# Filler matmuls of a planned attention and Fourier-mixing kernel: up to the first feed-forward products instead of nearly to the end

## The chip, the cores and the metric

The kernel runs on one core of one Trainium2 chip. Its time is measured on the device in microseconds; the number given is the median of several executions. One execution more is taken with the hardware profiler, and all rows of the profile are of that one.

## The reference

Inputs are q, k, v of shape (8, 12, 448, 64) and two weights, 768 x 3072 and 3072 x 768, in float32.

```python
q_n, k_n = q / |q|, k / |k|                       # along the 64
attn = softmax(q_n @ k_n.T / tau)                 # tau = 0.1
x = (attn @ v)  reshaped to (8, 448, 768)
u = x + real(fft(fft(x, axis=1), axis=2))
un = (u - mean(u)) / sqrt(var(u) + 1e-6)          # along the 768
out = u + relu(un @ w_ch1) @ w_ch2
```

## The kernel before

The kernel is not a loop that engines run through. It is a list of operations, each with the engines that can do it, its assumed duration, its priority, what it reads and writes, and the PSUM tiles that it takes. A planner puts them in order and the order is then written out for each engine, with a semaphore wait wherever an operation needs the result of another engine.

**The stages of a batch.** There are eight batches. For each: q and k rows are loaded into STG (three buffers), squared on ScalarE (L1371), summed on VectorE (L1373), their inverse norms made (L1170 to L1174), scaled on GpSimd into QH (L1384) and transposed by DMA into QK (L1390). Then come the scores (L1461, and L1474 for the rows that remain), the exponentials on ScalarE into E (L1439), the products with v (L1492, L1498) and the division by the row sums on VectorE into X (L1516, L1518). The Fourier transform is folded by its symmetries on VectorE into F and ACG (L1537 to L1589); a first set of products over the 448 rows (L1629) is copied out of PSUM by ScalarE (L1650) and VectorE (L1651), and a second set (L1679, L1682) makes the sums over the 768 columns, which VectorE adds to X to make U (L1713, L1724). Mean and variance follow, the normalized rows are written into F (L1776) and transposed by DMA into UNT (L1797). The feed-forward part multiplies UNT with W1b (the "up" products, named h, L1861), applies relu while it leaves PSUM into HQ (L1877; the first row tile of batch 0 goes into a part of TX), and multiplies with W2b (the "down" products, L2005). VectorE adds U on the way out (L2041, L2042), and SP or GpSimd stores the rows.

**How batches interleave.** Attention of batch b + 1 is listed ahead of the feed-forward part of batch b, and the planner weaves both together: products are put where TensorE would otherwise wait. W1b and W2b are loaded once by GpSimd's DMA queue during batch 0 (L1151, L1152), the 12 slices of W2b one behind the other. In batch 0 the down products of the first row tile run over both halves of the hidden columns, so that the last four of the first output half read the last W2b slice.

**The order.** `Plan.schedule` (L727) goes through simulated time with measured durations, a model of the DMA queues and a safety margin on DMA landings (for the weights, 1.5 us), and picks for each engine in turn the operation that can start first, by priority where several can. The order within an engine is fixed from then on.

**The fillers.** `Plan.fill` (L868) then walks TensorE's finished order. Wherever there is a gap of at least 0.36 us between two operations of the plan, within a stretch of planned time from t0 to t1, it can put in matmuls whose result nobody reads. Each filler is a group of six 128 x 128 x 128 matmuls (L2255), one for each 0.36 us of the gap (0.7 us early in the run), into a PSUM bank that is free in the plan at that time. A filler waits for the last VectorE operation that the plan has done by then, so that it doesn't run long before its time. With a `share` under 1, a gap is filled only where TensorE is busy for less than that share in some 3.4 us stretch around it. Nothing else moves: the order of the real operations stays, and no operation waits for a filler other than by standing behind it in TensorE's order.

`Kern.build` calls it twice (L2259, L2260). The first call goes from 7.5 us of the plan to `first`, the planned start of the first up product of batch 0 (`h0_0`), and multiplies an identity matrix that lies in TX. The second goes on from there and multiplies a piece of W1b, with a share of 0.75.

Of the kernel before, what the change touches and what calls it, by code (L numbers as in the profile page):

```python
# [970 lines left out]
class Kern:  # L971
# [1242 lines left out]
    def build(self):  # L2214
        self.stg_next = self.qh_next = self.ln_next = self.out_next = 0
        self.trs, self.loads, self.ssk, self.fd_ops, self.w, self.raw1, self.vl, self.pvs, self.exps = [], [], [], [], [], [], [], [], []
        self.first_st = self.main = self.last_qk = self.ldt = None
        self.units()
        self.hT0 = self.tf[:, 9216:12288].rearrange("p (f c) -> p f c", f=NF)
        self.snu, self.fs = [], []  # L2220
        self.consts()
        self.tables()
        self.attn(0)
        self.trig.order += tuple(self.exps)
        for b in range(self.nb):
            self.fft(b)
            if b == 0:
                self.weights(self.vl[2])
            if b + 1 < self.nb:
                self.attn(b + 1)  # L2230
            if b == 0:

                for c in range(3):
                    self.w[12 + c].deps.update(self.ssk)
                for c in (3, 4):
                    self.w[12 + c].deps.add(self.sqw)
                for c in range(5, 12):
                    self.w[12 + c].deps.update(self.raw1[3] + (self.raw1[4] if c > 7 else []))
            if b == self.nb - 2:
                self.s1 = []  # L2240
                self.wsums()
            self.ffn(b)
        seen = {}
        for op in self.P.ops:
            k = seen[op.name] = seen.get(op.name, -1) + 1
            op.prio = round(op.prio + SHIFT.get(op.name, {}).get(k, 0), 4)
            op.engs = (HOME[op.name][k],) if k in HOME.get(op.name, ()) else op.engs
        self.est = self.P.schedule()
        first = min(op.start for op in self.P.ops if op.name == "h0_0")

        def warm(w):
            def make(bank):
                def fn(pe):
                    for _ in range(6):
                        r = pe.matmul(self.PS[:, bank, 0:128], w, w, start=True, stop=True)  # L2255
                    return r
                return fn
            return make
        self.P.fill(7.5, first, self.id_op, warm(self.ID))  # L2259
        self.P.fill(first, self.est - 20.0, self.id_op, warm(self.W1b[:, 0, 0:128]), 0.75)  # L2260
        self.P.emit(self.nc, self.es)
        self.es.close()

# [52 lines left out]
```

## Time and profile before

| | us |
|---|---|
| median of 3 runs | 581.55 |
| lowest and highest run | 580.40 and 582.12 |
| the profiled execution | 580.54 |
| its span, first to last instruction | 578.7 |
| granted TensorE clock, mean over the span | 1.00 |
| TensorE matmuls busy | 557.1 |
| VectorE busy | 428.9 |
| ScalarE busy | 394.0 |
| GpSimd busy | 227.5 |

The profile's page gives the busy time of each engine, the span in 40 slices, the DMA queues, the chain of work that ended last, and the costliest groups of instructions. A group's row names line, engine and operation, what it writes and reads (out<-in), its shape and count, then busy time, the mean of one, and the idle time ahead of it with its releaser. In the order of time a row starts with the start and the length in us; what stands in brackets at its end is how long the engine sat idle ahead of it, and for whom. PE is TensorE, PEld its weight loads, DVE VectorE, ACT ScalarE, POOL GpSimd, SP the engine that issues DMAs. Matmuls are pipelined: a row's length runs to the end of its last matmul, and the next row can start before that.

### The profile page before, as it was taken

Reading aid. Unit: us, or ns where it says so; the run is one execution under the profiler, and the core shown is the slowest. Engines: PE = TensorE matmul, PEld = TensorE weight load, DVE = VectorE, ACT = ScalarE, POOL = GpSimd, SP = SyncE. Lnnn points to the kernel's source line nnn. Section 1 sums busy time; section 2 is a strip of 40 time slices with the busy share of each in tenths; the row PEclk is TensorE's granted clock in tenths of the full one; section 3 lists DMA queues with packets and bytes.
Section 4 is the critical chain, followed back from the end, with each engine's and each line's share of the span. In section 5 each row is a group of like instructions: output and inputs, shape, how many; then the busy total and the mean of one; then the engine's idle time right before and its main releaser. Section 6 shows DMA issues by size and latency. Waiting matters only on the chain.

```text
span 578.7 us, 16114 instructions
## 1 busy us (share of the span) xinstructions
PE 557.1 (96%) x6658; PEld 437.6 (76%) x6658; DVE 428.9 (74%) x917; ACT 394.0 (68%) x740; POOL 227.5 (39%) x332
## 2 busy tenths in 40 slices
PE   3899999989999999999999999999999999999997
PEld 3678787667688687868768688687786886969694
DVE  8889958778558957794698668866678469897262
ACT  7998875556777786767748877586565772857270
POOL 8523315157335634543371634645244002031303
PEclk9999999999999999999999999999999999999999
DMA  9999999995449766925495649561490300122001
GB/s 216 195 233 189 167 184 107 131 190 84 110 94 108 165 99 137 144 56 138 79 122 116 105 117 123 114 148 42 84 118 15 84 1 1 57 43 71 28 29 54
DMA packets 183946, 62.19 MB, mean 107 GB/s; under 512 B 166689, under 2 KB 181665, under 8 KB 183873
## 3 DMA queue, kind: packets, MB, share of 16 engines
q0 software_dynamic: 54048, 22.81, 34.7%
q1 hardware_dynamic: 129824, 38.35, 34.1%
q8 instruction: 52, 0.85, 0.6%
q14 instruction: 22, 0.17, 0.1%
HBM read 51.90 MB, written 11.01 MB: 109 GB/s over the span
## 4 chain that ended last, share of the span: by engine, by line
PE 80%; DVE 10%; ACT 4%; DMA 2%; POOL 2%; issue 1%; POOLq 0%; ACTq 0%; DVEq 0%
PE PS L2005 28%; PE PS L1861 27%; PE PS L1956 7%; PE PS L1498 5%; PE PS L1461 5%; ACT E L1439 2%; PE PS L1492 2%; PE PS L1474 1%; PE PS L2255 1%; DMA UNT<-F 1%; DVE SM L1250 1%; PE PS L1682 1%; PE PS L1629 1%; DMA QK<-QH 1%; DVE F L1544 1%
## 5 line engine op out<-in xcount | busy, mean ns | idle before, releaser
L1861 PE MATMUL PS<-UNT,W1b 128*128 128x256 bf16 (+1 forms) x1728 | 185.2, 264 | 3.0 <-DMA UNT<-F 2.2
L1861 PEld LDWEIGHTS PS<-UNT,W1b 128*128 128x128 bf16 x1728 | 153.8, 98 | 23.5 <-DMA UNT<-F 2.6
L1439 ACT ACTIVATE E<-PS 128x900 bf16<-128x900 f32 (+1 forms) x192 | 148.7, 826 | 28.7 <-PE PS L1461 23.4
L2005 PE MATMUL PS<-W2b,HQ 128*128 128x384 bf16 x720 | 125.5, 326 | 0.0
L1384 POOL TENSOR_TENSOR QH<-STG,SM 128x256 bf16<-128x256 f32 x126 | 88.2, 726 | 83.1 <-DVE SM L1174 56.6
L2005 PEld LDWEIGHTS PS<-W2b,HQ 128*128 128x128 bf16 x720 | 68.7, 98 | 43.4 <-issue 0.9
L2031 POOL TENSOR_TENSOR OUTB<-OUTB,U 128x192 f32<-128x192 f32 x72 | 51.9, 742 | 102.6 <-ACT OUTB L2026 100.8
L1877 ACT ACTIVATE HQ<-PS 128x512 bf16<-128x512 f32 x91 | 54.3, 597 | 43.0 <-PE PS L1861 40.6
L2005 PE MATMUL PS<-TX,HQ 128*128 128x384 bf16 (+2 forms) x444 | 76.8, 322 | 2.2 <-DVE OUTB L2042 2.2
L2005 PEld LDWEIGHTS PS<-TX,HQ 128*128 128x128 bf16 x444 | 41.6, 98 | 28.6 <-DVE OUTB L2042 3.6
L2105 DVE TENSOR_TENSOR HQ<-HQ 128x1536 bf16<-128x1536 bf16 (+1 forms) x73 | 52.8, 728 | 13.8 <-ACT HQ L1877 7.7
L1373 DVE TENSOR_REDUCE SM<-QH 128x6 f32<-128x384 f32 x84 | 45.5, 544 | 16.1 <-ACT QH L1371 15.8
L1371 ACT ACTIVATE QH<-STG 128x384 f32<-128x384 f32 x84 | 43.2, 518 | 13.2 <-DVE SM L1373 9.8
L1498 PE MATMUL PS<-VB,E 128*128 128x65 bf16 x1152 | 51.4, 193 | 0.0
L2064 POOL DMA_INDIRECT out_dram<-OUTB,IDX x21 | 22.5, 1073 | 67.6 <-DVE OUTB L2042 27.0
L1498 PEld LDWEIGHTS PS<-VB,E 128*128 128x128 bf16 x1152 | 47.7, 97 | 1.5
L1492 PE MATMUL PS<-VZ,E 128*128 128x130 bf16 x192 | 41.5, 219 | 0.6 <-ACT E L1439 0.5
L1877 DVE TENSOR_SCALAR HQ<-PS 128x512 bf16<-128x512 f32 x35 | 24.1, 688 | 22.6 <-PE PS L1861 22.3
L1416 POOL DMA_DIRECT2D VB<-in_v_dram x24 | 25.5, 1071 | 38.1 <-PE PS L1498 32.1
L1724 DVE SCALAR_TENSOR_TENSOR U<-ACG,X 128x768 bf16<-128x768 f32 (+4 forms) x39 | 39.5, 1020 | 0.8
L1461 PE MATMUL PS<-QK 64*128 64x225 bf16 (+2 forms) x864 | 39.5, 229 | 0.5 <-DMA QK<-QH 0.4
L2026 ACT ACTIVATE OUTB<-PS 128x384 f32<-128x384 f32 x36 | 17.5, 486 | 28.6 <-PE PS L2005 28.3
(193 smaller groups left out, 789.8 us busy)
## 6 DMA issues: line engine op xcount, KB each, us to landing
STG<-in_q_dram SPq DMA_DIRECT2D x18, 384.0 KB, 4.1
STG<-in_k_dram SPq DMA_DIRECT2D x18, 384.0 KB, 3.7
VB<-in_v_dram POOLq DMA_DIRECT2D x24, 192.0 KB, 6.6
W2b<-in_moe_w_ch_dram POOLq DMA_DIRECT2D x12, 384.0 KB, 7.4
W1b<-in_moe_w_ch_dram POOLq DMA_DIRECT2D x5, 768.0 KB, 11.9
out_dram<-OUTB SPq DMA_DIRECT2D x7, 384.0 KB, 3.8
W2b<-in_k_dram SPq DMA_DIRECT2D x2, 576.0 KB, 7.3
W2b<-in_q_dram SPq DMA_DIRECT2D x2, 576.0 KB, 10.1
```

The lines of the kernel that those rows point to most:

```text
L1371: P.add("act", lambda a, sq=sq, src=buf[:, w * x:w * x + w]: a.activation(sq, src, ACTF.Square), t_act(w), pr, f"sq{i}_{b}", reads=bn, wri ...
L1373: P.add("dve", lambda v, o=SS[:, i, H // ns * x:H // ns * (x + 1)], sq=sq: v.tensor_reduce(o, sq.rearrange("p (h d) -> p h d", d=DH), AX.X ...
L1384: r = v.tensor_tensor(v3(qh)[:, h:h + 4], v3(buf)[:, h:h + 4], RN[:, i, h:h + 4].unsqueeze(2).to_broadcast((128, 4, DH)), AluOp.mult)
L1439: return a.activation(o, self.PS[:, bk:bk + nc_, 0:SQ2], ACTF.Exp, scale=1.0 / self.tau)
L1461: i = pe.matmul(self.PS[:, bk + h, c0:c0 + n], self.KT[r, jj, kt * 128:(kt + 1) * 128], self.QT[r, jj, cols], start=True, stop=True)
L1492: r = pe.matmul(o, st(6), self.VZ[:, j, :], start=not split, stop=(split and i == 0), skip_group_check=True)
L1498: r = pe.matmul(o[:, 65 * h:65 * h + 65], st(2 * kt + h), self.VB[:, kt, 2 * j + h, :], start=(split and i == h == kt == 0), stop=((not sp ...
L1861: r = pe.matmul(self.PS[:, bk, x * n:(x + 1) * n], self.W1b[:, j, ft * 128:(ft + 1) * 128], self.UNT[:, j, cs], start=(j == 0), stop=(j == ...
L1877: return e.activation(o, i, ACTF.Relu) if e is self.nc.scalar else e.tensor_relu(o, i)
L2005: r = pe.matmul(self.PS[:, bk, 0:n], lhs(f), rhs(f), start=(start and f == 0), stop=(stop and f == NF // 2 - 1), skip_group_check=True)
L2031: r = g.tensor_tensor(self.OUTB[:, ob, xs], self.OUTB[:, ob, xs], self.U[:, ut, xs], AluOp.add)
L2105: P.add("dve", lambda v: v.tensor_tensor(cs(o), cs(a), cs(bq), op), 0.16 + 0.3 * len(ks), -0.5, f"{nm}{ks[0]}_{b}", reads=rd, writes=[x fo ...
```

## The change

One argument of the second call differs: the end of the stretch of planned time in which fillers may be put.

```diff
@@ -2257,7 +2257,7 @@
                 return fn
             return make
         self.P.fill(7.5, first, self.id_op, warm(self.ID))
-        self.P.fill(first, self.est - 20.0, self.id_op, warm(self.W1b[:, 0, 0:128]), 0.75)
+        self.P.fill(first, first + 12.0, self.id_op, warm(self.W1b[:, 0, 0:128]), 0.75)
         self.P.emit(self.nc, self.es)
         self.es.close()
 
```

`self.est` is the planned end of the last operation. The first call, the order of the real operations and their waits are the same.

## The prediction

> **What bounds the kernel now.** I read the page first, then the fillers' own line, then TensorE's order of time around them, then the chain of waits.
>
> ```profile
> span 578.7 us, 16114 instructions
> PE 557.1 (96%) x6658; PEld 437.6 (76%) x6658; DVE 428.9 (74%) x917; ACT 394.0 (68%) x740; POOL 227.5 (39%) x332
> ...
> PE 80%; DVE 10%; ACT 4%; DMA 2%; POOL 2%; issue 1%; POOLq 0%; ACTq 0%; DVEq 0%
> ```
>
> TensorE is busy for 96% of the span and carries 80% of the chain that ended last. A busy row is not proof of a bound, but the chain says the same: work taken off TensorE shortens the end, unless something else comes late in its place. So the questions are how much filler work really goes, and whether what follows it was ready.
>
> ```profile
> L2255 PE MATMUL PS<-TX x144: 217/219/314, 8.1 to 48.4; 128*128 128x128 bf16 x144
> L2255 PEld LDWEIGHTS PS<-W1b x60: 95/98/99, 93.9 to 97.7; 128*128 128x128 bf16 x60
> L2255 PE MATMUL PS<-W1b x60: 219/219/230, 94.0 to 97.7; 128*128 128x128 bf16 x60
> ```
>
> All fillers of the kernel are these: 144 from the first call (their operand lies in TX) and 60 from the second (operand W1b). The second call reaches nearly to the end of the plan, but it found only one place worth filling, 3.8 us wide, around 94 us.
>
> ```profile
> 48.66 6.81 PE L1861 MATMUL PS<-UNT,W1b 128*128 128x128 bf16 x114
> ```
>
> ```profile
> 92.71 1.46 PE L2005 MATMUL PS<-W2b,TX 128*128 128x384 bf16 x8
> 94.01 3.95 PE L2255 MATMUL PS<-W1b 128*128 128x128 bf16 x60
> 97.80 4.71 PE L2005 MATMUL PS<-W2b,TX 128*128 128x384 bf16 x28
> 102.34 0.56 PE L1629 MATMUL PS<-CS,F 128*97 128x225 bf16 x4
> ...
> 103.93 2.11 PE L2005 MATMUL PS<-W2b,HQ 128*128 128x384 bf16 x12
> 105.88 0.21 PE L1679 MATMUL PS<-CS,E 97*128 97x96 bf16 x1
> ```
>
> The first feed-forward product starts at 48.66 us. The new limit, 12 us later, is 60.7 us, and the 60 fillers lie 33 us beyond it: no disagreement of that size is likely between the plan's clock, in which the limit is counted, and the trace. Between 48.66 and 60.7 there is no filler now, and none can be added, since the lower bound of the stretch is the same. So the change is: all 60 go, nothing comes. The 144 stay. The row of the 28 products has no idle time ahead of it, so TensorE went straight from the fillers to them.
>
> ```profile
> 94.17 0.34 PE PS L2255 x6
> ...
> 94.52 3.44 PE PS L2255 x54
> 97.96 4.55 PE PS L2005 x28
> 102.51 1.58 PE PS L1629 x16
> 104.09 1.95 PE PS L2005 x12
> ```
>
> The chain runs through the fillers: 97.96 - 94.17 = 3.79 us. That is the largest gain, 0.65% of the run. A change of 0.3% (1.74 us) is about what a measurement of this kernel can tell from no change.
>
> **Term 1: were the 28 products ready at 94.01?** They read the last slices of W2b, the results of earlier products, and a PSUM bank.
>
> ```profile
> 86.18 0.71 POOL L1152 DMA_DIRECT2D W2b<-in_moe_w_ch_dram  x1 [8.95 <-DMA W2b<-in_moe_w_ch_dram]
> ```
>
> ```profile
> W2b<-in_moe_w_ch_dram POOLq DMA_DIRECT2D x1, 384.0 KB, 4.5
> ```
>
> ```profile
> 93.00:94.00 1.00, 1.00 (x8) 0.57 (x6) 1.00 (x4) 0.04 (x1) 1.00 (x3) 1.00 0.00 0
> 94.00:95.00 1.00, 0.99 (x15) 0.70 (x14) 0.97 (x3) 0.89 (x2) 0.38 (x1) 1.00 0.00 0
> ```
>
> The twelfth and last W2b load is issued at 86.18 and lands 4.5 us later, at 90.7. The windows say the same (their columns: stretch, length, busy time and count of PE, weight loads, VectorE, ScalarE and GpSimd, granted clock, DMA share, GB/s): the DMA engines moved nothing from 93 to 95 us. So the slice that the planner expected late is there 3.3 us before TensorE reaches the gap. The plan has a wait there of the fillers' length; on the chip it doesn't exist, and the fillers only delay.
>
> ```profile
> 89.08 0.68 DVE L1877 TENSOR_SCALAR HQ<-PS 128x512 bf16<-128x512 f32 x1
> ...
> 97.90 0.64 DVE L1589 TENSOR_TENSOR F<-ACG 128x388 bf16<-128x388 bf16 x2
> ...
> 99.84 0.30 DVE L1174 RECIPROCAL SM<-SM 128x24 f32<-128x24 f32 x1
> ```
>
> The last eviction of a feed-forward bank (L1877) is over by 89.76, so the bank and the operand are free too. Term 1: the 28 products start at 94.01 instead of 97.80, gain 3.79, and end (4.55) at 98.56. What hides the W2b load is the work ahead of 94 us; each microsecond of landing beyond 94.0 would cost one.
>
> **Term 2: the sums of the transform, L1629.** They come next and need the fold that VectorE ends with L1589, at 97.90 + 0.64 = 98.54. VectorE doesn't wait for the fillers (they wait for it), so this time doesn't move.
>
> ```profile
> 41.64 1.27 DVE SM L1250
> 42.95 0.84 PE PS L2255 x12
> ```
>
> The handover from VectorE to TensorE costs 42.95 - 41.64 - 1.27 = 0.04, and a weight load may be uncovered for 0.098. So L1629 starts between 98.56 and 98.54 + 0.14 = 98.68, against 102.34: gain 3.66 to 3.78.
>
> **Term 3: the second transform, L1679.** It needs the evictions of L1629 by ScalarE (L1650) and VectorE (L1651).
>
> ```profile
> 102.55 0.62 DVE L2041 SCALAR_TENSOR_TENSOR OUTB<-PS,MV,U 128x384 f32<-128x384 f32 x1 [2.40 <-PE PS L2005]
> ...
> 103.08 0.54 DVE L1373 TENSOR_REDUCE SM<-QH 128x6 f32<-128x384 f32 x1
> ...
> 103.34 0.92 ACT L1650 ACTIVATE E<-PS 128x900 bf16<-128x900 f32 x1 [3.32 <-PE PS L1629]
> ...
> 104.13 1.09 DVE L1651 CAST E<-PS 97x900 bf16<-97x900 f32 x1 [0.51 <-PE PS L1629]
> ...
> 107.14 1.03 DVE L1713 TENSOR_TENSOR ACG<-PS,ACG 128x388 f32<-128x388 f32 x2 [1.45 <-PE PS L1682]
> ```
>
> VectorE's order behind L1174, which ends at 100.14 by a chain that doesn't hang on the fillers, is L2041, L1373, L1651: 100.14 + 0.62 + 0.54 + 1.09 = 102.39, and with the handover 102.53. TensorE itself would be there at 98.68 + 1.58 + 1.95 = 102.21. So VectorE ends last by about 0.3 us, and L1679 starts at 102.53 against 105.88: gain 3.35 (3.66 if the three overlap as closely as L2041 and L1373 do now). ScalarE has waited 3.32 us for its part and has the room. I take 3.4.
>
> **Term 4: all that follows.** From L1713 on VectorE waits for TensorE again. Its three waits for TensorE in this stretch are 2.40 + 0.51 + 1.45 = 4.36 us, more than the 3.79 removed, so it can follow. The next place where something other than TensorE ends last is this:
>
> ```profile
> 105.31 4.67 SPq L1390 DMA_TRANSPOSE QK<-QH  x2
> ...
> 114.69 5.78 SPq L1797 DMA_TRANSPOSE UNT<-F  x3
> ...
> 122.95 3.23 PE L1861 MATMUL PS<-UNT,W1b 128*128 128x256 bf16 x28 [2.20 <-DMA UNT<-F]
> ```
>
> ```profile
> 111.00:112.00 1.00, 1.00 (x9) 0.61 (x7) 1.00 (x3) 0.39 (x1) 0.00 (x0) 1.00 0.29 61
> 112.00:113.00 1.00, 1.00 (x8) 0.61 (x7) 0.93 (x5) 0.94 (x4) 0.00 (x0) 1.00 0.00 0
> ```
>
> TensorE waits 2.20 us for the transposes of batch 1's normalized rows, which hang on L1713 and so move with it. Issued 3.4 us earlier, at 111.3, they meet an SP queue that is free since 105.31 + 4.67 = 109.98 and DMA engines that fall idle during that very microsecond (0.29 busy, then 0.00). At most 0.3 us is lost; the 2.20 us wait stays as it is. From there on every load is set off by a buffer that comes free, and each engine has waited for TensorE, so all is shifted alike. No wait is added, no DMA is moved; those that hang on TensorE's count behind the gap come earlier with it.
>
> **Sum.** 3.79 less 0.4 is 3.4 us. The profiled execution took 580.54 us (span 578.7 and 1.84 around it) and would take 577.1; it lies 1.0 below the median of the runs, 581.55, which becomes 578.1.
>
> **A rule that speaks against it.** The granted clock is 1.00 in every window above, with the fillers in. But the rows of the start show what fillers are for:
>
> ```profile
> 8.06 2.74 PE L2255 MATMUL PS<-TX 128*128 128x128 bf16 x24 [8.06 <-DVE SM L1250]
> 11.43 1.46 PE L2255 MATMUL PS<-TX 128*128 128x128 bf16 x12 [0.63 <-DVE SM L1173]
> ```
>
> After 8.06 us without work, twelve matmuls take 1.46 us, where the same twelve take 0.84 at 42.95. The Trainium skill, TensorE: Matmul & The Clock Gate, section "Why this matters for your kernels", says that the array must not idle for more than some 3 us between bursts, since one idle window drops its clock to half. By that rule a 3.8 us hole at 94 us would be paid for behind it. The slow rows agree with its direction, though the clock column reads 1.00 there as well. It bites only if the hole stays open, and by term 1 the products close it.
>
> **Rivals.** *Slower: the hole stays open and the clock falls.* Place: 94.0 to 97.8 us. It decides if the last W2b slice lands some 3 us or more after 94.0, that is 6 us later than in the profile; then nothing is gained by the removal, and the matmuls behind run slowly. Price by the start's rows: the slow pace lasted at least from 8.06 to 11.43 + 1.46 = 12.89, 4.83 us, and at 0.84 instead of 1.46 us per twelve they would have taken 2.78, so 2.05 lost: 583.6. For it: the planner did expect to wait. Against: the landing at 90.7, and DMA engines at rest.
>
> *No change: the gain is given back at the UNT transposes.* If those didn't come earlier, because their queue or an engine in front of them keeps its time, TensorE would wait there 2.20 + 3.4 = 5.6 us and the run stay at 581.5; half given back leaves 579.8. For it: this is the one wait of over 2 us behind the gap, so nothing spare covers a delay there. Against: the queue and the engines are free in the rows of term 4.
>
> *The edit does nothing:* it would if the planned place lay within 12 us of the first product; the trace has it 45 us behind. Then 581.55.
>
> **How the numbers follow.** Forecast 0.85 (gain over 1.74 us, most likely 3.4), given back 0.09, no effect 0.02, slower 0.04. So faster 0.85, same 0.11, slower 0.04. The range: full gain of 3.79 with a median as far under as the lowest run shown is now (1.15) gives 576.6; above, half given back with the same median's 0.57 over (the highest run, 582.12) gives 580.4.
>
> **What would show it.** Right: 204 fillers become 144, none behind 48.4; L2005 x28 right after 94.0 without idle time; L1629 near 98.7, L1679 near 102.5 with a short wait for VectorE's L1651, the UNT wait still about 2.2 us at 119.5, granted clock 1.00. Wrong: TensorE idle at 94 to 98 us with products at a slower pace behind it (term 1), a wait for UNT of over 4 us (term 4), or a new wait for QK later that the 3.4 us uncovered.

## The result, and the profile after

| | before | after |
|---|---|---|
| median of all runs, us | 582.02 (17 runs) | 575.65 (17 runs) |
| lowest and highest run | 580.40 and 583.74 | 574.49 and 580.28 |
| the profiled execution | 580.54 | 576.17 |
| after over before | | 0.9898, interval 0.9883 to 0.9913 |

The kernel became faster by 5.9 us (5.1 to 6.8). The forecast had the sign, and the fillers' removal as the forecast described it is there, with 3.7 us. It was too low: it had 3.4 us of gain, and 3.79 as the most that the fillers could give. About 2 us came from a place where it had expected nothing.

The page of after, its first rows: 120 instructions on TensorE fewer, 60 matmuls and their 60 weight loads.

```profile
span 574.2 us, 15994 instructions
PE 553.6 (96%) x6598; PEld 433.3 (75%) x6598; DVE 428.4 (75%) x917; ACT 393.4 (69%) x740; POOL 227.6 (40%) x332
```

The fillers' own line in after: the first call's 144 are left, and none lies behind 48.5 us.

```profile
L2255 PE MATMUL PS<-TX x144: 216/219/314, 8.1 to 48.5; 128*128 128x128 bf16 x144
```

TensorE's order of time in after, around the place (start, length, then in brackets the idle time ahead of the row and its releaser):

```profile
92.72 6.01 PE L2005 MATMUL PS<-W2b,TX 128*128 128x384 bf16 x36
98.61 0.60 PE L1629 MATMUL PS<-CS,F 128*97 128x225 bf16 x4
...
102.21 0.20 PE L1679 MATMUL PS<-CS,E 97*128 97x96 bf16 x1
...
117.42 12.84 PE L1861 MATMUL PS<-UNT,W1b 128*128 128x256 bf16 x116 [0.34 <-DMA UNT<-F]
```

The 8 products ahead of the fillers and the 28 behind them are now one row of 36 without a break. L1629 starts 3.73 us earlier than before (98.61 against 102.34) and L1679 3.67 (102.21 against 105.88). Then comes the row that the forecast didn't have: the products on UNT wait 0.34 us for the transposes, not 2.20, and start 5.53 us earlier than in before (117.42 against 122.95).

**Where the lead grows and shrinks.** All engines execute the same instructions in the same order in both kernels, the 120 apart, so each instruction of TensorE can be set against its twin. The table gives the start in after less the start in before, at five places of before's time, for two profiled executions of after (the second is e7 below):

| at, us of before | after | after again (e7) |
|---|---|---|
| 109.9 | -3.68 | -3.43 |
| 122.95, UNT | -5.53 | -5.27 |
| 139.9, QK | -6.02 | -5.77 |
| 199 | -6.49 | -6.40 |
| the end | -4.47 | -5.55 |

The first row is the fillers. The second adds 1.85 us at the UNT transposes. The third adds 0.5 at a wait for QK transposes which stood in before, in its order of time,

```profile
139.92 0.56 PE L1461 MATMUL PS<-QK 64*128 64x225 bf16 x8 [0.43 <-DMA QK<-QH]
```

and has no idle time in after; the section on more counts comes back to it. Where the 0.5 us between 140 and 199 us come from stays open. Part of the lead is given back later, and not alike in two executions of the same kernel. The largest single piece, in after alone, is this row of its order of time, which e7 does not have:

```profile
233.91 3.67 PE L1861 MATMUL PS<-UNT,W1b 128*128 128x256 bf16 x30 [0.59 <-ACT HQ L1877]
```

**What happened to the 2.20 us.** VectorE and ScalarE work between 107 and 121 us of before's time comes 3.67 to 3.73 us earlier in after, and so do the three transpose issues:

```profile
111.02 5.68 SPq L1797 DMA_TRANSPOSE UNT<-F  x3
```

against 114.69 in before: 3.67. So the issue explains none of the extra 1.85. The landing does. The products wait for one semaphore, that of the second of these transposes, and the chain of before has that wait as a step of its own (start, length):

```profile
117.30 5.60 DMA UNT<-F
```

The second transpose, issued at 117.30, landed at 122.90, and TensorE went on at 122.95. In after it was issued at 113.58 (3.72 us earlier), its semaphore had the last of its 16 updates at 117.38, and TensorE went on at 117.42. From issue to landing it took 5.60 us in before and 3.80 in after: 1.80 us less. The first transpose isn't what TensorE waits for (in before it landed in 2.8 us), and neither is the third (4.45 us, at 123.66, when TensorE had gone on).

What else was on the DMA engines while TensorE stood still? The DMA view of before, from 120.6 to 122.9 us (queue, then packets, MB, share):

```profile
DMA packets 680, 0.19 MB, mean 81 GB/s; under 512 B 679, under 2 KB 679, under 8 KB 679
...
q1 hardware_dynamic: 679, 0.17, 121.4%
q8 instruction: 1, 0.02, 2.5%
```

and of after, in its own stop from 116.9 to 117.4 us:

```profile
DMA packets 422, 0.11 MB, mean 216 GB/s; under 512 B 422, under 2 KB 422, under 8 KB 422
...
q1 hardware_dynamic: 422, 0.11, 113.1%
```

One packet tells them apart: a single 16 KB packet of the queue named "instruction". Both pages have 52 of them:

```profile
q8 instruction: 52, 0.85, 0.6%
```

0.85 MB over 52 is 16384 bytes. The trace has 13,445 records of TensorE in before and 13,325 in after, so one packet is 256 instructions of 64 bytes (52 x 256 = 13,312). In before the first of the 52 begins when TensorE has started 281 instructions and the last when it has started 13,234, which is 254 from one to the next: these are TensorE's instructions being fetched. The Trainium skill, Runtime: NRT & Kernel Launch, section "Instruction fetch mechanics", says that a sequencer refills its buffer in blocks of 16 KiB, 256 instructions, by a DMA queue of its own, and that crossing a block's end is mostly hidden. The block's size agrees with the rows above. What a crossing costs TensorE's own stream no row here shows; the packets below show who else pays.

The trace has every packet. The 256-byte packets of the transposes, from the first UNT issue until TensorE goes on:

```
                        fetch            packets over 0.6 us   they start       they end         longest
before                  120.95-121.89    18 of 2354            121.14-121.27    122.68-122.72    1.56 us
before again (e4)       122.07-123.01    18 of 2352            122.25-122.39    123.80-123.84    1.57 us
after + 120 (e1)        121.85-122.78    20 of 2521            122.14-122.17    123.58-123.61    1.44 us
after                   none              0 of 2375                                              0.21 us
fillers kept (e6)       none              0 of 2186                                              0.09 us
```

The median packet takes 18 ns. In the three executions with a fetch, 18 to 20 packets that start some 0.2 to 0.3 us behind its start all end together, 0.8 us after its end. The semaphore that TensorE waits for moves with them: in before the first of its 16 updates comes at 121.61, the other fifteen from 122.74 to 122.90, right behind the end of these packets; in after all sixteen come from 117.19 to 117.38. How the fetch holds the packets, and these the semaphore, the trace doesn't tell.

The rest of the run shows the same. Of the 52 fetches of before, 8 have 16 to 25 such long packets beside them, each time with a DMA transpose on its way, and those packets end 0.8 to 0.9 us behind the fetch. Beside the fetches at 29.82, 84.60, 281.25 and 388.03 us, where packets of 256 bytes passed with no transpose on its way, none was long. In all 15 traces together no fetch without a transpose on its way has one.

### The profile page after: what moved, and what is told of

Same layout as the page of the kernel before. It is cut to its first block, busy times and chain, and to the rows that moved or that the text cites. A ratio compares the mean times of both kernels' runs of the same rounds, so it can differ in the third digit from the quotient of the medians.

```text
span 574.2 us, 15994 instructions
## 1 busy us (share of the span) xinstructions
PE 553.6 (96%) x6598; PEld 433.3 (75%) x6598; DVE 428.4 (75%) x917; ACT 393.4 (69%) x740; POOL 227.6 (40%) x332
## 4 chain that ended last, share of the span: by engine, by line
PE 58%; DVE 5%; DMA 1%; ACT 1%; issue 1%; SPq 0%; POOLq 0%; DVEq 0%; ACTq 0%
PE PS L2005 22%; PE PS L1861 18%; PE PS L1956 7%; PE PS L1461 4%; PE PS L1498 3%; DMA QK<-QH 1%; PE PS L1492 1%; PE PS L1474 1%; ACT E L1439 1%; PE PS L1625 1%; PE PS L1682 1%; DVE F L1544 1%; SPq L1390 0%; DVE OUTB L2042 0%; DVE U L1724 0%
## 5 line engine op out<-in xcount | busy, mean ns | idle before, releaser
L2064 POOL DMA_INDIRECT out_dram<-OUTB,IDX x21 | 22.9, 1089 | 65.1 <-DVE OUTB L2042 27.0
```

## The experiments

Three theories were set against each other on the extra 2 us, beside the 3.7 of the fillers. **A**: an instruction fetch fell beside the UNT transposes in before and doesn't in after, and what moved it is the count of TensorE's instructions ahead (120 fewer). **B**: the earlier start of everything, or the fillers' absence itself, did it. **C**, formed on the way, when the count failed: the fetch is the cause wherever it falls, but the count alone doesn't place it. None of the edits changes an output: a filler's result is read by nobody.

### The count put back, and taken away: e1, e2, e4

e1 is after with 120 instructions that only test a semaphore already reached, ahead of TensorE's first operation (two waits make one instruction):

```diff
+                if e == "pe":
+                    for _ in range(240):
+                        eng.wait_ge(sems["dve"], 1)
```

> The kernel after, with 120 semaphore instructions more at the very start of TensorE's stream (waits that are met at once, in the 8 us in which TensorE has nothing to do). So each instruction stands at the same place of the stream as before the change, without the 60 fillers. Theory A (removal of the fillers is worth 3.7 us, the other 2 to 2.7 us come from where TensorE's 16 KB instruction fetches fall: 256 instructions each, and the change moved all that follow by 120): the wait for the UNT transposes comes back, about 2 us at 119 us, and the time is 582.0 - 3.7 = 578.3, ratio 0.993 to 0.995. Theory B (the earlier start itself makes the transposes land sooner, whatever the instruction count): as after the change, wait 0.3 us, time 575.7, ratio 0.989 to 0.990.

e2 is before with 136 of them (`range(272)`), which with the 120 of the fillers makes 256, one fetch more:

> The kernel before, fillers and all, with 136 such semaphore instructions at the start: 120 + 136 = 256, so the fetches fall at the same instructions as in the kernel after, one fetch later. Theory A: 575.7 + 3.7 = 579.4, ratio 0.995 to 0.997, and the wait for UNT at 121 us shrinks from 2.2 to about 0.3 us. Theory B: as before, 582.0, ratio 0.999 to 1.001, wait 2.2 us.

e4 is before again:

> The kernel before once more, for a second trace. Theory A: an instruction fetch runs again at 120 to 122 us beside the UNT transposes, whose last lands 4 us or more after its issue, and TensorE waits 2 us or more for it. Theory B says nothing of the fetch; the wait is 2.2 us.

e1 took 580.99 us, ratio 1.0008 (0.9993 to 1.0022); e2 584.69, 1.0071 (1.0049 to 1.0094); e4, executed once, 582.05. The times of e1 and e2 can't be read as intended, because the added instructions aren't free. e1's order of time begins

```profile
13.88 0.37 PE L2258 MATMUL PS<-TX 128*128 128x128 bf16 x2 [13.88 <-DVE SM L1177]
```

where after begins at 8.06. The records of these tests start 0.106 us one behind the other. But the waits can be read. Order of time of e1 (its lines are numbered three higher), then the DMA view of that stop:

```profile
123.84 1.50 PE L1864 MATMUL PS<-UNT,W1b 128*128 128x256 bf16 x9 [2.13 <-DMA UNT<-F]
```

```profile
q1 hardware_dynamic: 690, 0.17, 127.5%
q8 instruction: 1, 0.02, 2.5%
```

There isn't a filler behind the start in e1, and the wait is back, with a fetch in it, and a landing of 5.59 us. Something else came with it. TensorE was busy for 38% of the 3.41 us up to 124.51, and for the next 3.41 us it had half its clock. The windows behind the wait, of e1 and of before:

```profile
124.50:128.00 3.50, 3.50 (x19) 2.52 (x17) 2.19 (x3) 0.60 (x1) 2.02 (x2) 0.51 1.21 225
```

```profile
123.60:127.10 3.50, 3.50 (x34) 3.13 (x33) 2.26 (x3) 1.21 (x3) 1.68 (x2) 1.00 1.21 225
```

The profiled execution of before had no such fall, though behind 20 us TensorE is nowhere less busy over 3.4 us than around this wait (36%).

e2 has all 204 fillers, and its view of TensorE's waits says

```profile
PE PS L1864 <- DMA UNT<-F: 0.3, 1, 0.3
```

The wait went with the fetch both times, against the fillers: B fails, since the fillers' absence is neither enough (e1) nor needed (e2). Both kernels start late, so this alone leaves time as a way out for B. e4 shows that the wait in before is no accident of one execution:

```profile
124.07 1.16 PE L1861 MATMUL PS<-UNT,W1b 128*128 128x256 bf16 x9 [2.16 <-DMA UNT<-F]
```

### The hole left open: e3

The prediction's slower rival was a hole of the fillers' length with nothing in it. e3 is after, in which the product that stood behind the fillers waits for a VectorE operation that ends at 97.9 us:

```diff
+        late = [op for op in self.P.order["pe"] if op.name == "y001_0"][2]
+        late.deps.add([op for op in self.P.order["dve"] if op.name == "g1_1"][1])
```

> The kernel after, in which the product that followed the fillers waits for the VectorE operation (L1572, the later of two) that ends about when they ended: an open hole of some 3.7 us in place of the fillers, with the instruction count of the kernel after. This is the rival of the prediction made true. If the clock holds, the 3.7 us are lost and nothing else: 579.4 by theory A (ratio 0.995 to 0.997), 582.0 by theory B (0.999 to 1.001). If the clock falls behind the hole, 2 us more: 581.4 by theory A, 584 by theory B, granted clock under 1.00 and matmuls at about 1.7 times their spacing behind 98 us.

580.22 us, ratio 1.0004 (0.9985 to 1.0022), with runs from 577.97 to 582.2. Its waits of TensorE, and the windows at and behind the hole (stretch, length, busy time and count of PE, weight loads, VectorE, ScalarE and GpSimd, granted clock, DMA share, GB/s):

```profile
PE PS L2005 <- DVE ACG L1572: 3.7, 1, 3.7
```

```profile
94.00:98.00 4.00, 0.28 (x3) 0.14 (x3) 3.93 (x10) 1.54 (x4) 3.25 (x5) 1.00 0.71 144
98.00:102.00 4.00, 4.00 (x26) 2.43 (x25) 1.88 (x6) 0.95 (x3) 3.18 (x5) 1.00 3.85 115
```

In the profiled execution the products behind the hole start 3.78 us later than in after, its own length, and nothing is lost beyond: the clock reads 1.00 behind 3.7 us of idle time. The rule quoted in the prediction (the Trainium skill, TensorE: Matmul & The Clock Gate, section "Why this matters for your kernels") has it fall; in this execution it didn't. This execution, 577.97, is the lowest of e3's runs, though. By the ratios e3 lies 1.0004 - 0.9898 = 0.0106 of 580, 6 us, above after. The mean clock of each run tells where part of the rest went: it is 1.00 in the two shortest runs (577.97 and 578.31) and 0.996 or 0.997 in the other ten, whose median is 580.7. One stretch of 3.41 us at half clock, the shortest that a trace here shows ahead of the kernel's end, takes 1.7 us of 576 off the mean, which gives 0.997. So in ten of twelve runs the clock fell once, in agreement with that rule, and they took some 2.5 us longer. That it fell behind the hole is likely but not shown: none of the ten has a trace.

### The early fillers taken out as well: e8

```diff
-        self.P.fill(7.5, first, self.id_op, warm(self.ID))
+        pass
```

> The kernel after without the early fillers too (the first call left out): no matmul is put in anywhere. 288 instructions less, so fetches fall within 32 instructions of where they fall in the kernel after. If the early fillers keep the clock up for work that TensorE waits on, products ahead of 48 us run at 1.7 times their spacing for some us and the time is 1 to 3 us above the kernel after; if ScalarE and VectorE bound the start, as their busy shares of 8 to 9 tenths there say, it is the same within 1 us. Theories A and B say nothing on it.

578.86 us, ratio 0.996 (0.9945 to 0.9976): 3.3 us above after on the same chip (e7, 575.59). The windows of e8, then of after:

```profile
45.00:50.00 5.00, 5.00 (x34) 4.69 (x32) 3.87 (x15) 3.23 (x3) 1.40 (x2) 0.50 1.25 208
50.00:55.00 5.00, 4.30 (x45) 4.07 (x44) 4.30 (x11) 3.49 (x11) 1.76 (x2) 0.55 1.17 206
```

```profile
45.00:50.00 5.00, 4.87 (x67) 4.07 (x66) 4.96 (x18) 4.40 (x9) 1.40 (x2) 1.00 1.24 208
50.00:55.00 5.00, 4.88 (x88) 4.71 (x86) 4.77 (x18) 4.11 (x12) 2.03 (x3) 1.00 1.09 193
```

Here the clock does fall to half, for 10.24 us, and from 45 to 50 us TensorE, busy throughout, starts 34 matmuls where after starts 67; at 50 us of before's time it is 3.80 us late. The fall to half is what the Trainium skill, TensorE: Matmul & The Clock Gate, section "Why this matters for your kernels", gives; the idle stretch of some 3 us that the quoted rule asks for wasn't there. TensorE's longest wait between 14 us and the fall was 1.4 us, and it was busy for 43% of the last 3.41 us. So fillers have a worth, in the start, where TensorE is thinly used; where the 60 at 94 us stood, products were ready.

### The count changed without delaying the start: e5, e6, e7

Some of the early groups of six 128 x 128 matmuls become groups of ten or eleven 64 x 64 ones, which take about as long. e6 does it to before, 17 groups by 4 more matmuls (68 matmuls, 136 instructions), all fillers kept:

```diff
-        def warm(w):
+        def warm(w, more=iter(())):
...
-                    for _ in range(6):
-                        r = pe.matmul(self.PS[:, bank, 0:128], w, w, start=True, stop=True)
+                    for c in (lambda x: [64 if x else 128] * (6 + x))(next(more, 0)):
+                        r = pe.matmul(self.PS[0:c, bank, 0:c], w[:, 0:c], w[:, 0:c], start=True, stop=True)
...
-        self.P.fill(7.5, first, self.id_op, warm(self.ID))
+        self.P.fill(7.5, first, self.id_op, warm(self.ID, iter([4] * 17)))
```

> The kernel before with its 60 fillers at 94 us, in which 17 early filler groups hold 10 matmuls of 64 x 64 in place of 6: 136 instructions more, which with the 120 are 256, one fetch. Fetches fall at the same work as after the change. Theory A: wait for UNT about 0.3 us near 121, time 2 us or so under the kernel before, ratio 0.995 to 0.998. Theory B: wait 2.2 us, ratio 0.999 to 1.001.

578.75 us, ratio 0.9961 (0.9949 to 0.9974), that is 2.2 us faster than before, with every filler in. Its order of time and the DMA view of the stop (120.9 to 121.6 us):

```profile
121.58 1.69 PE L1861 MATMUL PS<-UNT,W1b 128*128 128x256 bf16 x14 [0.50 <-DVE F L1776]
```

```profile
DMA packets 579, 0.15 MB, mean 212 GB/s; under 512 B 579, under 2 KB 579, under 8 KB 579
...
q1 hardware_dynamic: 579, 0.15, 114.2%
```

No fetch, the second transpose landed 3.85 us after its issue, and 0.50 us of wait. Its start is 0.33 us late, and at 122.95 it is 1.37 ahead of before: 1.70 gained at UNT; at 140 it is 1.88 ahead, so 0.5 more at QK.

e5 does the same to after (12 groups of 11, 120 instructions, the fillers' number):

> The kernel after, in which 12 of the early filler groups hold 11 matmuls of 64 x 64 in place of 6 of 128 x 128: 120 instructions more in TensorE's stream, as many as the change took out, put ahead of 40 us in gaps in which TensorE waits anyway, so that the start isn't delayed as by the semaphore instructions of the first two experiments. Instruction fetches fall where they fell before the change. Theory A: wait for UNT about 2.1 us near 119, gain against the kernel before 3.7 us, ratio 0.993 to 0.995. Theory B: wait 0.3 us, ratio as the kernel after on the same chip.

and e7 is after again:

> The kernel after once more, on the same chip as the other two, for the ratio and a second trace. Theory A: wait for UNT about 0.3 us at 117 us and no fetch beside the last UNT transpose; ratio 0.989 to 0.992. Theory B: the same.

e7: 575.59, 0.9912 (0.989 to 0.9935), wait 0.4. e5: 576.48, 0.9926 (0.9905 to 0.9948), wait 0.5. A had wanted e5's wait back at 2.1. The fetch that should have fallen into the stop came at 120.65, after TensorE had gone on at 118.97. It began when TensorE had started 2777 instructions, where before, e4 and e1 have 2744 each. A's strict form fails here; the missing fetch and the missing wait still go together.

These three kernels on one chip take the gain apart: before 580.99; with the fetch moved out of the wait but all fillers kept, 578.75 (e6); with the fillers gone too, 575.59 (e7). By the medians that is 2.2 us for the fetch and 3.2 for the fillers.

The clock is in these medians too. Of the 23 runs of before on this chip, 12 have a mean clock of 0.997 or less and a median of 582.25; the 11 with 0.999 or 1.00 have 580.45. Of e6's 12 runs one has 0.997, of e7's 6 two have 0.994. With the runs of 0.999 and 1.00 alone, before has 580.45, e6 578.83 and e7 574.97: 1.6 us for the fetch and 3.9 for the fillers, near the 1.70 and 3.7 of the traces. That the falls of before lie behind its UNT wait, as in e1, is likely but not shown, since no run of before with a fall has a trace. If they do, the wait costs more than its length.

### More counts: e9, e10, e11, e12, e13

The same edit with other lists (and with `64 if x > 0`, so that shorter groups keep 128 x 128): e9 is after with `[4] * 15` (+120 instructions), e10 with `[4] * 8` (+64), e11 with `[-2] * 16` (16 groups of only four, -64).

> The kernel after with 15 early filler groups of 10 matmuls of 64 x 64 in place of 6 of 128 x 128: 120 instructions more, as in the fifth experiment, but in smaller groups, which delayed the start by 0.3 us in the sixth where the fifth's larger ones delayed it by 1.5. Fetches fall at the same work as in the kernel before, and the start is nearly undisturbed. Theory A, taken strictly: the fetch runs beside the last UNT transpose again, which lands 4.4 us after its issue, the wait for UNT is about 2.1 us, and the ratio 0.993 to 0.996. If the wait stays under 0.6 us as in the fifth experiment, the instruction count alone doesn't set the time of the fetch, and the ratio is 0.990 to 0.992.

> The kernel after with 64 instructions more at the start (8 early groups of 10 small matmuls): fetches a quarter of a block earlier than in the kernel after. Theory A: times between the placings differ by up to 2 us with where fetches meet transposes; no value can be said beforehand, 0.988 to 0.996. Theory B: as the kernel after, 0.989 to 0.992, since the work starts at the same time.

> The kernel after with 64 instructions less at the start (16 early groups of 4 matmuls in place of 6): fetches a quarter of a block later. Theory A: 0.988 to 0.996, by where they meet transposes. Theory B: 0.989 to 0.992. If the shorter early groups let the clock fall, the granted clock of the stretch up to 50 us shows it.

e9: 575.37, 0.9891 (0.9874 to 0.9908). e10: 576.09, 0.9917 (0.9893 to 0.9941). e11: 575.24, 0.988 (0.9861 to 0.9898). All three intervals overlap with after's. None has a fetch in the stop, none a long wait. e9 again has the count of before and its fetch only at 118.70 (after 2763 instructions), 0.9 us after TensorE went on:

```profile
117.82 2.34 PE L1861 MATMUL PS<-UNT,W1b 128*128 128x256 bf16 x20 [0.50 <-issue]
```

So the count alone doesn't place the fetch, and A is given up for C.

**The wait for QK is a second case.** e5 and e9 have no fillers at 94 us, and e9 starts only 0.2 us later than after. Yet in both a fetch falls beside the transpose that TensorE needs at QK: it begins at 133.26 in e5 and at 132.04 in e9, the transpose lands 4.4 and 4.6 us after its issue, and TensorE waits, 0.33 us in e5 and in e9

```profile
134.92 0.57 PE L1461 MATMUL PS<-QK 64*128 64x225 bf16 x8 [0.57 <-DMA QK<-QH]
```

The kernel before, e4 and e1 have the same there: a fetch, landings of 4.6 to 4.7 us and waits of 0.43 to 0.56. In the other ten traces no fetch falls among its packets, it lands after 2.7 to 2.8 us, and TensorE doesn't wait. So the extra 0.5 us of after at this place have the same cause as the 1.85 at UNT.

e12 tests C against B with before itself, all 204 fillers at first and then 8 of the early groups cut to four matmuls (`[-2] * 8`, 32 instructions fewer):

> The kernel before with its 60 fillers and 32 instructions less at the start (8 early filler groups of 4 matmuls in place of 6): the fetch that ran in TensorE's wait for UNT at 121 us would come 32 instructions later in the work, that is after the wait. Theory C (the extra gain is a matter of whether a fetch falls between the issue and the landing of the last UNT transpose, and the place of the fetch shifts with the count of instructions and with some 30 instructions of its own history): wait 0.3 to 0.7 us, ratio 0.994 to 0.998, fillers and all. Theory B (the earlier start makes them land sooner): wait 2.2 us, ratio 0.999 to 1.001.

577.75 us, 0.9929 (0.9903 to 0.9956). In its order of time TensorE doesn't wait for UNT at all:

```profile
121.87 3.33 PE L1861 MATMUL PS<-UNT,W1b 128*128 128x256 bf16 x29
```

The fetch is at 125.26, and the second transpose landed in 2.78 us. That is a microsecond under the 3.8 of after, and this part is not the fetch: in e12 and e11 GpSimd's store (L2064) was issued 1.73 us ahead of this transpose, in the other 13 traces only 1.1 us ahead. Its packets of 6 KB pass directly before the transpose's, which in before and after start 2.0 us behind the issue, in e12 and e11 1.0 us. 16 matmuls fewer in the start of before, and 4.4 us are gained by the medians; the ratio is just under the 0.994 to 0.998 that C had given. The clock has a part here too: it is 1.00 in all six runs of e12, and 0.997 or less in four of the eleven of before, 582.26 us and more. The profiled execution, 580.29, was the longest of its runs, so its trace accounts for only part of that: TensorE is 1.3 us behind before from the start on, 1.08 ahead behind the UNT wait (2.4 gained there), 1.5 ahead behind QK, and gives it all back in the second half. C expected the wait to go, B to stay.

e13 tried the reverse, a fetch put back into after's stop, by `[4] * 19` (+152):

> The kernel after with 152 instructions more at the start (19 early groups of 10 small matmuls): 32 more than in the ninth experiment, in which the fetch came 0.9 us after TensorE had gone on. 32 instructions are 16 products of 0.16 us, so the fetch should come some 1 to 2 us before TensorE stops, beside the last UNT transpose. Theory C: that transpose lands 3.5 to 4.5 us after its issue, the wait is 1 to 2.2 us, and the ratio 0.992 to 0.996, without fillers. Theory B: wait under 0.6 us, ratio 0.988 to 0.991.

575.28 us, 0.9887 (0.9861 to 0.9913). The fetch fell at 113.88 to 114.82, while the second transpose was being issued (114.10) and no packet of 256 bytes started; that transpose landed in 3.79 us and the wait was 0.5. It wasn't placed where it was meant to be, so it tests nothing, except that a fetch in the pause between the packets of two transposes costs nothing.

**All executions beside each other.** TensorE's idle time before the UNT products, the time from issue to landing of the second transpose, and the fetch next to it:

| | idle, us | landing | fetch in it | wait |
|---|---|---|---|---|
| before | 120.75 to 122.95 | 5.60 | 120.95 to 121.89 | 2.20 |
| before (e4) | 121.91 to 124.07 | 5.62 | 122.07 to 123.01 | 2.16 |
| after + 120 (e1) | 121.71 to 123.84 | 5.59 | 121.85 to 122.78 | 2.13 |
| after | 117.08 to 117.42 | 3.80 | none | 0.34 |
| after (e7) | 117.32 to 117.68 | 3.82 | none | 0.36 |
| after, hole (e3) | 120.77 to 121.28 | 3.80 | none | 0.50 |
| after, no fillers (e8) | 120.66 to 121.15 | 3.79 | none | 0.49 |
| after, +120 (e5) | 118.48 to 118.97 | 3.79 | none | 0.49 |
| after, +120 (e9) | 117.32 to 117.82 | 3.79 | none | 0.50 |
| after, +64 (e10) | 117.00 to 117.49 | 3.78 | none | 0.49 |
| after, +152 (e13) | 117.49 to 117.98 | 3.79 | none | 0.49 |
| after, -64 (e11) | 117.42, none | 2.75 | none | 0 |
| before, +136 (e2) | 127.20 to 127.55 | 3.81 | none | 0.35 |
| before, +136 (e6) | 121.08 to 121.58 | 3.85 | none | 0.50 |
| before, -32 (e12) | 121.87, none | 2.78 | none | 0 |

The late rows matter: e3, e8, e6 and e12 reach this place at 120.7 to 121.9, as late as before, and don't wait long. Neither the time of day nor the fillers go with the long wait. The fetch does, in each row. Where TensorE waits at all, it goes on 0.04 to 0.1 us behind that landing, also where its row names another releaser (e6, e9). GpSimd's store doesn't: it was issued 1.1 us ahead in the rows of 5.6 us and in those of 3.8 alike.

## Why the prediction was wrong

**Terms 1 to 3 held.** The 28 products were ready: the row of 36 has no idle time in it, and L1629 came 3.73 us earlier, inside the 3.66 to 3.78 that were given. In term 3 VectorE's L1651 was taken to end last, with L1679 at 102.53; it started at 102.21, the time that the text gave for TensorE alone. VectorE's three operations overlap as closely as the text allowed for in brackets, so this term was 0.3 us too small. The fillers' worth is 3.7 us in the trace, and 3.2 between e6 and e7 by the medians.

**Term 4 is the step that failed**: "At most 0.3 us is lost; the 2.20 us wait stays as it is." The wait became 0.34 us, so 1.86 more were gained there, 0.5 at the QK wait behind it, and 0.5 by 199 us. The issue of the transposes moved just as the text said (3.67 us earlier, and the queue was free); the time from issue to landing did not stay. The text took it as the transfer's own. Of the 5.60 us, 3.80 are there without a fetch as well, and 1.80 came from an instruction fetch beside it. The sign could have been found in before: of equal transposes the first landed in 2.8 us and the second, issued 2.6 us later, in 5.60, and such a difference wants a cause. The fetch, one packet of 52, was in the DMA view of that stop.

**The range** failed for the same reason. Its low end, 576.6, was the full gain of the fillers with a low median; the measured 575.65 lies under it. The one wait of over 2 us behind the place was weighed as something that could grow (a rival had it at 5.6 us), but not as something that could shrink. "All is shifted alike" was also too simple for the rest of the run: of 6.5 us of lead at 199 us, 0.9 to 2.0 were given back by the end in the two traces, which hides part of what was gained. By the medians 5.9 us were gained and by the traces 4.5 to 5.5; a clock that fell in many runs of before on the chips of the experiments, and in neither of its traces, can make up part of the difference.

**The rivals.** The hole wasn't open. Opened on purpose (e3), it cost its length in the trace and no more. The price of a fallen clock, 2.05 us in the prediction, wasn't paid in that execution, but the ten runs with a lower mean clock took some 2.5 us longer than the two without, so a price of that size is borne out. The 1.00 in the clock column over the first microseconds, which the prediction read beside this rule, is no reading: the clock records of before's trace begin at 16.36 us. The gain wasn't given back at UNT. The edit did what it says.

**What stays open** is what sets the moment of a fetch. The fetch in question began when TensorE had started 2744 instructions in before, e4 and e1, 2739 to 2741 in after, e7 and e3, but 2777 and 2763 in e5 and e9, whose count ahead is that of before. The fetch and the second transpose meet or miss each other within a few microseconds. That the fetch is the cause rests on 15 traces, at two places: three long waits at UNT and five short ones at QK, each with a fetch beside the transpose, and none without. At UNT no kernel without fillers and without a late start had the fetch put back (e5, e9 and e13 missed); at QK e9 is such a kernel, with a start 0.2 us late. By which step the fetch holds the packets is not shown.

## What to carry to other kernels

When an engine waits for a transfer, ask first why that transfer took as long as it did: set its time from issue to landing against its equals, and look what else the DMA engines carried in that stretch, instructions among it. A wait that is over the transfer's own time isn't a fixed part of the kernel; any edit that adds or removes instructions ahead of it can take it away or bring it, so a range should let it go both ways. And an edit that changes the number of instructions is to be compared with a kernel that changes the number alone (e6, e12), or the gain is put down to the wrong thing.

## What the runs showed of the hardware

- TensorE's instructions come by DMA in packets of 16 KB, 256 instructions each, 52 in before and in after; one takes 0.9 to 1.7 us in before, up to 2.1 in after. With a DMA transpose on its way, 18 to 20 packets of 256 bytes that started 0.2 to 0.3 us behind the start of the fetch ended together 0.8 us after its end, up to 1.57 us after their own start, where the median packet takes 18 ns. One such meeting cost TensorE 1.7 to 1.9 us at UNT and 0.3 to 0.6 at QK.
- The second UNT transpose landed in 2.75 and 2.78 us where GpSimd's store was issued 1.73 us ahead of it (e11, e12), in 3.8 where it was issued 1.1 us ahead, and in 5.6 with a fetch as well.
- A semaphore test that is already met isn't free on TensorE: 120 of them, 0.106 us one behind the other, held the first matmul until 13.88 us (e1).
- Where a trace shows the granted clock fall to 0.50 before the end of the kernel, TensorE had been busy for 38% (e1), 49% (after, at 14.46 us) and 43% (e8) of the 3.41 us ahead; it stayed low for 3.41, 3.41 and 10.24 us. Idle for 3.7 us at 94 us it kept 1.00 in the profiled execution of e3, and had a mean of 0.996 or 0.997 in ten of the twelve runs.
- The kernel before itself had medians of 579.96 to 582.12 us on the chips used here, so that the ratios above are with runs of before on the same chip, taken with those of the run compared.
